# Moving a clamp from VectorE to GpSimd and putting a one-element ScalarE write ahead of each attention exponential

## The chip, the cores and the metric

The kernel runs on one core of one Trainium2 chip. The metric is the device time of one execution in microseconds (us). A core has five engines that each run their own list of instructions in order and meet through semaphores: TensorE (PE, matmuls; its weight loads are shown as PEld), VectorE (DVE), ScalarE (ACT), GpSimd (POOL) and SyncE (SP, which here only issues DMAs). Matmuls write to PSUM, which has eight banks; everything else on the chip lies in SBUF.

## The reference

Two attention blocks with separate inputs, whose results are laid side by side. Each has sequence S = 2048, width D = 640 and 32 heads of 20.

```python
def _A_ref(x, wqkv, wo):            # sliding window of 256
    q, k, v = split(x @ wqkv)       # (B, H, S, 20) each
    scores = einsum("bhqd,bhkd->bhqk", q, k) * 20 ** -0.5
    scores = where((0 <= i - j) & (i - j < 256), scores, -1e9)
    return merge(einsum("bhqk,bhkd->bhqd", softmax(scores), v)) @ wo

def _B_ref(x, wqkv, wo):            # linear attention
    q, k, v = split(x @ wqkv)
    phi = lambda t: where(t > 0, t + 1, exp(t)) + 1e-6
    pq, pk = phi(q), phi(k)
    kv, z = einsum("bhsd,bhse->bhde", pk, v), pk.sum(axis=2)
    num, den = einsum("bhqd,bhde->bhqe", pq, kv), einsum("bhqd,bhd->bhq", pq, z)
    return merge(num / (den[..., None] + 1e-6)) @ wo

concatenate([_A_ref(A), _B_ref(B)], axis=-1)
```

The kernel computes phi(t) as max(t, 0) + min(exp(t) + 1e-6, 1 + 1e-6): the second term is the clamp that the change is about.

## The kernel before

**Units of block A.** The window attention is cut into 90 units: for a piece `s` of 512 queries and a group `g` of four heads there are two or three units, each with up to 512 score columns for each of the four heads. `scores` (line 474) runs a unit: 8 to 16 matmuls (line 483) write S_ps, a tile of four PSUM banks of which there is one; one exponential on ACT (line 491) turns all 128x2048 scores into a tile `p`, of which there are three; one or two `affine_select` instructions on POOL (line 505) set to zero what lies outside the window. `values` (line 516) multiplies `p` by v (line 527) into O_ps, one PSUM bank of which there is one, and after the last unit of a group DVE divides by the row sums (lines 549 and 550). `values` of a unit is issued two units after its `scores` (LAG = 2).

**Fill.** Everything else (the projections of A and B, block B, both output projections) is a generator, `fill` (line 627), of dense matmuls. The loop over the units (line 672) issues `scores` of the unit, `values` of the unit two before, and then so many columns of `fill` as a credit allows, about 3,715 a unit. The order on every engine is what this program order gives; nothing is reordered later. TensorE thus runs, unit by unit: scores, older values, about one and a half dense chains. A dense chain (line 194) is five matmuls that add up in one of three PSUM banks (tile `dense`); DVE, or in `phi` ACT and DVE, has to read a bank before a later chain can write it.

**phi** (line 200) takes a bank `src`: ACT writes `e = exp(src)` (line 203); DVE clamps `e` in SBUF (line 207); DVE adds max(src, 0), which reads the bank a last time (line 210, a `scalar_tensor_tensor`, "the sum" below). The two DVE instructions are not issued at once but kept in `later`, and issued by the next `flush`, that is right behind the next eviction or the next phi's exponential. phi runs 40 times, five at a time: in the four `b_kv(s)` (keys of B, each chain followed by one of v) and the four `b_q(s)` (queries of B).

**Who else uses POOL.** Besides the selects it sets a column of ones in v (lines 309 and 358), masks kv (line 163, once, ten instructions) and issues the DMAs of line 106, 617 and 349, all in one order.

Of the kernel before, what the change touches and what calls it, by code (L numbers as in the profile page):

```python
# [9 lines left out]
P = 128  # L10
ALU = mybir.AluOpType
ACT = mybir.ActivationFunctionType
ENG = mybir.EngineType
BF16 = mybir.dt.bfloat16
# [6 lines left out]
SB = 512  # L21
# [31 lines left out]
def kernel(  # L53
# [10 lines left out]
    nc = tc.nc  # L64
# [4 lines left out]
    scale = float(DH) ** -0.5  # L69
# [5 lines left out]
    def pool(name, bufs, space=None):  # L75
        if space is None:
            return ctx.enter_context(tc.tile_pool(name=name, bufs=bufs))
        return ctx.enter_context(tc.tile_pool(name=name, bufs=bufs, space=space))
# [6 lines left out]
    pp = pool("p", 3)  # L85
# [3 lines left out]
    op1 = pool("o1", 2)  # L89
# [59 lines left out]
    ident = wp.tile([P, P], BF16, name="ident")  # L149
# [26 lines left out]
    def flush():  # L176

        while later:
            later.pop(0)()
# [20 lines left out]
    def phi(dst, src, view=lambda t: t[:]):  # L200

        e = sp.tile([P, SB], BF16, name="e")
        nc.scalar.activation(out=view(e), in_=src, func=ACT.Exp)  # L203
        flush()

        def rest():
            nc.vector.tensor_scalar(  # L207
                out=e[:], in0=e[:], scalar1=1e-6, scalar2=1.0 + 1e-6, op0=ALU.add, op1=ALU.min
            )
            nc.vector.scalar_tensor_tensor(  # L210
                out=dst, in0=src, scalar=0.0, in1=view(e), op0=ALU.max, op1=ALU.add
            )

        later.append(rest)
# [140 lines left out]
    def b_kv(s):  # L355
# [4 lines left out]
        def done(tb, ps):  # L360
            if tb is None:
                phi(pk[:, :, SB:D], ps, lambda t: t[:].rearrange("p (t n) -> p t n", n=P))
            else:
                phi(pk[:, tb, 0:SB], ps[:])
# [45 lines left out]
    def b_q(s):  # L410
        xt = xB[NS + s]
        pq = pqp.tile([P, KT, SB], BF16, name="phi")
        pq_of[s] = pq
        for c in range(KT):
            ps = bank()
            yield from chain(
                ps[:],
                lambda kt: w_sb["B"][:, kt, c * P : (c + 1) * P],
                lambda kt: xt[:, kt, :],
                SB,  # L420
            )
            phi(pq[:, c, :], ps[:])
            yield End(SB)
# [47 lines left out]
    def key(s, rel):  # L471
        return 4 * s + rel

    def scores(s, parts):
        S_ps = sps.tile([P, 4, SB], F32, name="S_ps")
        p = pp.tile([P, 4, SB], BF16, name="p")
        for g, rel, blk, qs in parts:
            kb = key(s, rel)
            kt = k_pad[kb // TPS]
            ko = (kb % TPS) * P  # L480
            q0, n = qs[0][0] * P, len(qs) * P
            for j in range(4):
                nc.tensor.matmul(  # L483
                    S_ps[:, j, blk * P : blk * P + n],
                    lhsT=kt[32 * j : 32 * j + DH, g, ko : ko + P],
                    rhs=q_pad[s][32 * j : 32 * j + DH, g, q0 : q0 + n],
                    start=True,
                    stop=True,
                    tile_position=(32 * j, 0),
                )  # L490
        nc.scalar.activation(out=p[:], in_=S_ps[:], func=ACT.Exp, scale=scale)  # L491
        runs = []
        for _, _, blk, qs in sorted(parts, key=lambda x: x[2]):
            for i, (_, kind) in enumerate(qs):
                if kind == "F":
                    continue
                b = blk + i
                if runs and runs[-1][0] == kind and runs[-1][2] == b:
                    runs[-1][2] = b + 1
                else:  # L500
                    runs.append([kind, b, b + 1])
        for kind, b0, b1 in runs:
            v = p[:, :, b0 * P : b1 * P].rearrange("p j (b q) -> p j b q", q=P)
            sgn = 1 if kind == "D" else -1
            nc.gpsimd.affine_select(  # L505
                out=v,
                in_=v,
                pattern=[[0, 4], [0, b1 - b0], [sgn, P]],
                compare_op=ALU.is_ge,
                fill=0.0,  # L510
                base=0 if kind == "D" else -1,
                channel_multiplier=-sgn,
            )
        return p
# [157 lines left out]
    for i, (okey, first, last, parts) in enumerate(units):  # L672
        p = scores(okey[0], parts)
        if i == 0:
            late_loads()
        pend.append((okey, first, last, parts, p))
        if len(pend) > LAG:
            values(*pend.popleft())
        credit += rate
        credit -= take(credit)  # L680
# [35 lines left out]
```

## Time and profile before

| what | us |
|---|---|
| median of 3 runs (lowest, highest) | 291.31 (289.54, 292.64) |
| the profiled execution's own time | 290.37 |
| its span (first to last instruction of the program) | 288.5 |
| TensorE busy | 273.9 (95%) |
| ScalarE busy | 193.4 (67%) |
| VectorE busy | 183.5 (64%) |
| GpSimd busy | 161.0 (56%) |

All times inside the execution are counted from the span's start. The granted TensorE clock was full throughout. In the groups of instructions a line reads: source line, engine, operation, tiles out<-in, shapes, xcount | busy time of the group, mean ns of one | idle time of the engine just before them <- what ended it. Busy time of TensorE contains pipelining with modelled ends, so 95% does not by itself mean that TensorE is the limit.

Some more numbers of this profile. TensorE waits for DVE to free a dense bank for 0.9 + 0.2 us (line 210), 1.8 us (line 449) and 1.7 us (line 185) in all; it waits 0.5 us for the exponential of line 491. The first exponential starts at 38.65 us and the last at 269.14 us. The clamp on DVE takes 282, 373 and 1409 ns (lowest, median, highest of 40) and 530 on the mean; the sum behind it 692 ns; the exponential of line 203 takes 591 ns. On POOL a select over 512 elements takes 690 ns on the mean, one over 1024 elements 1114 ns.

### The profile page before, as it was taken

How to read it: one execution, taken by the hardware profiler on the slowest of the kernel's cores; microseconds unless marked ns; L12 is line 12 of the kernel's file. 1: busy time of each engine (PE TensorE's matmuls, PEld its weight loads, DVE VectorE, ACT ScalarE, POOL GpSimd, SP SyncE). 2: the span in 40 equal slices, each digit the busy share in tenths (PEclk: the TensorE clock that was granted, in tenths of full speed). 3: DMA queues.
4: the chain of work that ended last, by engine and by line, in shares of the span. 5: the costliest groups of instructions: out<-in, count | busy, mean ns of one | idle time of the engine just before them, and what ended most of it. 6: DMA issues, size and time to landing. Idle time of an engine off the chain costs nothing.

```text
span 288.5 us, 8169 instructions
## 1 busy us (share of the span) xinstructions
PE 273.9 (95%) x3512; PEld 159.1 (55%) x3512; DVE 183.5 (64%) x409; ACT 193.4 (67%) x137; POOL 161.0 (56%) x212
## 2 busy tenths in 40 slices
PE   7999999999999999999999899998999999998995
PEld 7644555665666644565654554444545464545653
DVE  0666646847855744556657884458866887677861
ACT  2000058978889777789888767797688878976402
POOL 2000039657576666776699556666665766665620
PEclk9999999999999999999999999999999999999999
DMA  7997699999173172362062543079755145022486
GB/s 245 291 320 197 166 197 251 269 107 207 36 118 70 24 69 93 94 138 46 2 128 59 113 49 114 4 179 151 129 113 72 70 70 137 2 93 48 130 168 204
DMA packets 66676, 35.91 MB, mean 124 GB/s; under 512 B 50801, under 2 KB 65265, under 8 KB 66641
## 3 DMA queue, kind: packets, MB, share of 16 engines
q1 hardware_dynamic: 63792, 27.04, 49.5%
q0 software_dynamic: 1536, 7.05, 7.7%
q10 hardware_dynamic: 1312, 1.31, 1.4%
q8 instruction: 27, 0.44, 0.6%
q14 instruction: 9, 0.07, 0.1%
HBM read 12.45 MB, written 10.49 MB: 79 GB/s over the span
## 4 chain that ended last, share of the span: by engine, by line
PE 58%; ACT 17%; DVE 9%; issue 6%; DMA 6%; POOL 2%; SPq 0%; ACTq 0%; POOLq 0%
PE dense L194 35%; ACT p L491 14%; PE S_ps L483 10%; PE O_ps L527 9%; DMA k_scr<-st 2%; ACT e L203 2%; DMA kpad<-k_scr 2%; DVE phi L210 2%; PE dense L377 2%; DMA oT<-otokA 2%; PE dense L146 2%; DVE e L207 1%; POOL p L505 1%; DVE osb L185 1%; DVE otokB L449 1%
## 5 line engine op out<-in xcount | busy, mean ns | idle before, releaser
L491 ACT ACTIVATE p<-S_ps 128x2048 bf16<-128x2048 f32 x90 | 169.0, 1878 | 72.9 <-PE S_ps L483 68.2
L505 POOL TENSOR_SCALAR_AFFINE_SELECT p<-p 128x512 bf16<-128x512 bf16 (+2 forms) x178 | 145.1, 838 | 112.3 <-ACT p L491 112.2
L527 PEld LDWEIGHTS <-p 128*128 128x128 bf16 x1440 | 42.4, 96 | 19.7 <-issue 16.2
L527 PE MATMUL O_ps<-vA,p 128*128 128x21 bf16 x1440 | 51.1, 173 | 0.8 <-POOL p L505 0.7
L194 PE MATMUL dense<-wB,xB 128*128 128x320 bf16 (+2 forms) x320 | 49.3, 298 | 0.2 <-DVE phi L210 0.2
L194 PE MATMUL dense<-xA,wA 128*128 128x512 bf16 x200 | 46.1, 379 | 0.0
L185 DVE CAST st<-dense 128x512 bf16<-128x512 f32 x40 | 27.4, 690 | 20.5 <-PE dense L194 18.7
L483 PE MATMUL S_ps<-qpad,kpad 20*128 20x256 bf16 (+2 forms) x736 | 36.1, 269 | 2.9 <-ACT p L491 0.5
L185 DVE CAST osb<-dense 128x512 bf16<-128x512 f32 (+1 forms) x39 | 25.2, 647 | 16.1 <-PE dense L194 16.0
L194 PEld LDWEIGHTS <-xA 128*128 128x128 bf16 x320 | 26.4, 97 | 15.6 <-issue 1.5
L194 PEld LDWEIGHTS <-xB 128*128 128x128 bf16 x320 | 26.1, 97 | 13.3 <-issue 1.2
L483 PEld LDWEIGHTS <-kpad 20*128 20x128 bf16 x736 | 15.0, 92 | 32.4 <-issue 29.2
L194 PEld LDWEIGHTS <-wA 128*128 128x128 bf16 x200 | 18.5, 97 | 19.6
L210 DVE SCALAR_TENSOR_TENSOR phi<-dense,e 128x512 bf16<-128x512 f32 x40 | 27.7, 692 | 1.4
L194 PE MATMUL dense<-woA,oT 128*128 128x512 bf16 (+1 forms) x160 | 25.8, 299 | 2.7 <-DVE osb L185 1.6
L207 DVE TENSOR_SCALAR e<-e 128x512 bf16<-128x512 bf16 x40 | 21.2, 530 | 11.2 <-ACT e L203 11.1
L194 PE MATMUL dense<-xB,wB 128*128 128x512 bf16 x100 | 25.7, 378 | 0.9 <-DVE phi L210 0.8
L194 PE MATMUL dense<-wA,xA 128*128 128x320 bf16 x160 | 24.9, 299 | 1.4 <-DVE otokB L449 0.8
L194 PE MATMUL dense<-woB,xA 128*128 128x512 bf16 (+1 forms) x160 | 25.3, 299 | 0.5 <-PE dense L436 0.4
L203 ACT ACTIVATE e<-dense 128x512 bf16<-128x512 f32 x40 | 23.4, 593 | 0.2 <-PE dense L194 0.2
L185 DVE CAST vB<-dense 128x320 bf16<-128x320 f32 x32 | 15.2, 488 | 11.5 <-PE dense L194 11.1
L549 DVE RECIPROCAL recA<-O_ps 128x16 f32<-128x16 f32 (+1 forms) x34 | 8.5, 250 | 20.8 <-PE O_ps L527 20.7
(35 smaller groups left out, 152.0 us busy)
## 6 DMA issues: line engine op xcount, KB each, us to landing
out_dram<-osb POOLq DMA_DIRECT2D x7, 640.0 KB, 3.9
qpad<-q_scr SPq DMA_DIRECT2D x16, 160.0 KB
kpad<-k_scr SPq DMA_DIRECT2D x16, 160.0 KB
wA<-in_A_wqkv_dram SPq DMA_DIRECT2D x3, 800.0 KB
q_scr<-st SPq DMA_DIRECT2D x3, 640.0 KB
k_scr<-st SPq DMA_DIRECT2D x3, 640.0 KB
wB<-in_B_wqkv_dram SPq DMA_DIRECT2D x2, 800.0 KB
wB<-in_B_wqkv_dram POOLq DMA_DIRECT2D x1, 800.0 KB, 10.8
```

The costliest lines, as they stand in the source:

```text
L146: nc.tensor.matmul(ps[:, 0:P], lhsT=ident[:], rhs=ident[:], start=True, stop=True)
L185: nc.vector.tensor_copy(out=dst, in_=src)
L194: nc.tensor.matmul(dst, lhsT=lhs(kt), rhs=rhs(kt), start=(kt == 0), stop=(kt == KT - 1))
L203: nc.scalar.activation(out=view(e), in_=src, func=ACT.Exp)
L207: nc.vector.tensor_scalar(out=e[:], in0=e[:], scalar1=1e-6, scalar2=1.0 + 1e-6, op0=ALU.add, op1=ALU.min)
L210: nc.vector.scalar_tensor_tensor(out=dst, in0=src, scalar=0.0, in1=view(e), op0=ALU.max, op1=ALU.add)
L377: nc.tensor.matmul(pv, lhsT=pk[:, tb, c * P : (c + 1) * P], rhs=vB[:, tb, a : b + 1, :], start=(tb == 0), stop=(tb == TPS - 1),)
L483: nc.tensor.matmul(S_ps[:, j, blk * P : blk * P + n], lhsT=kt[32 * j : 32 * j + DH, g, ko : ko + P], rhs=q_pad[s][32 * j : 32 * j + DH, g, ...
L491: nc.scalar.activation(out=p[:], in_=S_ps[:], func=ACT.Exp, scale=scale)
L505: nc.gpsimd.affine_select(out=v, in_=v, pattern=[[0, 4], [0, b1 - b0], [sgn, P]], compare_op=ALU.is_ge, fill=0.0, base=0 if kind == "D" el ...
L527: nc.tensor.matmul(O_ps[:, slot, j, :], lhsT=p[:, j, b * P : (b + 1) * P], rhs=v_tok[kb // TPS][:, kb % TPS, 4 * gg + j, :], start=(first ...
L549: nc.vector.reciprocal(out=r[:, 0:n, :, :], in_=O_ps[:, :, :, DH:HV])
```

## The change

The clamp is issued on POOL instead of DVE, and it is issued at once behind the exponential of `phi`, no longer through `later`; the sum stays in `later` and on DVE. The tile `p` becomes two elements wider, and in front of the score matmuls of each unit ACT copies one element (of the identity matrix `ident`) into the first extra element of the new `p`. The exponential writes the first 2048 elements as before. The copy adds 90 instructions to ACT; the clamp takes 40 from DVE and adds 40 to POOL.

```diff
         e = sp.tile([P, SB], BF16, name="e")
         nc.scalar.activation(out=view(e), in_=src, func=ACT.Exp)
+        nc.gpsimd.tensor_scalar(
+            out=e[:], in0=e[:], scalar1=1e-6, scalar2=1.0 + 1e-6, op0=ALU.add, op1=ALU.min
+        )
         flush()
 
         def rest():
-            nc.vector.tensor_scalar(
-                out=e[:], in0=e[:], scalar1=1e-6, scalar2=1.0 + 1e-6, op0=ALU.add, op1=ALU.min
-            )
             nc.vector.scalar_tensor_tensor(
                 out=dst, in0=src, scalar=0.0, in1=view(e), op0=ALU.max, op1=ALU.add
             )
...
         S_ps = sps.tile([P, 4, SB], F32, name="S_ps")
-        p = pp.tile([P, 4, SB], BF16, name="p")
+        p_all = pp.tile([P, 4 * SB + 2], BF16, name="p")
+        p = p_all[:, 0 : 4 * SB].rearrange("p (j q) -> p j q", j=4)
+        nc.scalar.activation(out=p_all[0:1, 4 * SB : 4 * SB + 1], in_=ident[0:1, 0:1], func=ACT.Copy)
...
-        nc.scalar.activation(out=p[:], in_=S_ps[:], func=ACT.Exp, scale=scale)
+        nc.scalar.activation(out=p, in_=S_ps[:], func=ACT.Exp, scale=scale)
```

In the built program the exponential of line 491 waits for TensorE, ScalarE and GpSimd before the change (an event instruction of ACT holds the first two waits, the exponential the third), from the fifth unit on. After it, the one-element copy holds the waits for the old readers and writers of `p`, and the exponential waits for TensorE alone.

## The prediction

> **What bounds the kernel now.** I read the page's first part, then its groups, then ACT's instructions in order of time, then the chain that ended last, and last the timeline of one unit.
>
> ```profile
> PE 273.9 (95%) x3512; PEld 159.1 (55%) x3512; DVE 183.5 (64%) x409; ACT 193.4 (67%) x137; POOL 161.0 (56%) x212
> L491 ACT ACTIVATE p<-S_ps 128x2048 bf16<-128x2048 f32 x90 | 169.0, 1878 | 72.9 <-PE S_ps L483 68.2
> L207 DVE TENSOR_SCALAR e<-e 128x512 bf16<-128x512 bf16 x40 | 21.2, 530 | 11.2 <-ACT e L203 11.1
> ```
>
> TensorE looks full, and ACT waits 68.2 us for scores. But ACT's instructions in order of time (start, duration) show a beat:
>
> ```profile
> 41.02 1.88 ACT L491 ACTIVATE p<-S_ps 128x2048 bf16<-128x2048 f32 x1 [0.50 <-PE S_ps L483]
> 42.80 0.59 ACT L203 ACTIVATE e<-dense 128x512 bf16<-128x512 f32 x1
> 43.40 1.88 ACT L491 ACTIVATE p<-S_ps 128x2048 bf16<-128x2048 f32 x1
> ...
> 51.42 1.88 ACT L491 ACTIVATE p<-S_ps 128x2048 bf16<-128x2048 f32 x1
> 53.20 0.59 ACT L203 ACTIVATE e<-dense 128x512 bf16<-128x512 f32 x1
> 53.88 1.88 ACT L491 ACTIVATE p<-S_ps 128x2048 bf16<-128x2048 f32 x1
> ```
>
> From 51.42 to 53.88 is 2.456 us, and 51 of the 89 intervals of the 90 exponentials go with that beat: there the next scores begin 0.05 us behind the exponential's end. There is one S_ps, so exponential, scores, exponential is a closed loop. In the other 38 intervals TensorE comes to the scores later than that. So two limits alternate, TensorE's own work per unit and this loop, and TensorE has on the mean 0.12 us to spare in the 51. The chain shows what lies between scores and exponential:
>
> ```profile
> 242.13 0.36 PE S_ps L483 x8
> 242.49 0.02 issue
> 242.51 0.04 ACTq L491
> 242.55 0.04 issue
> 242.59 1.89 ACT p L491
> ```
>
> ACTq L491 is the event instruction that holds the wait for the scores. 41.02 to 43.40 is the beat of the first units, whose exponentials wait for TensorE alone: 2.375 us, 0.08 less. Third, phi, in the timeline of one unit:
>
> ```profile
> 73.48 0.59 ACT L203 ACTIVATE e<-dense 128x512 bf16<-128x512 f32 x1
> ...
> 73.65 1.78 POOL L505 TENSOR_SCALAR_AFFINE_SELECT p<-p 128x1024 bf16<-128x1024 bf16 x2 [1.14 <-ACT p L491]
> ...
> 74.11 0.79 DVE L207 TENSOR_SCALAR e<-e 128x512 bf16<-128x512 bf16 x1 [0.59 <-ACT e L203]
> ...
> 74.93 0.69 DVE L210 SCALAR_TENSOR_TENSOR phi<-dense,e 128x512 bf16<-128x512 f32 x1
> 75.68 0.37 PEld L194 LDWEIGHTS <-xB 128*128 128x128 bf16 x3 [0.21 <-issue]
> ```
>
> The sum (line 210) ends at 75.63 and the next chain in the same bank starts at 75.68. I paired each of the 40 sums with the next chain in its bank (the built program tells the bank): 12 chains start 0.05 us behind the sum, four more within 0.26 us. TensorE now waits only about 1 us for it in all, because the sum comes just in time.
>
> **The change, part by part.**
>
> *The exponential's waits.* With TensorE alone to wait for, the loop is 0.08 us shorter. TensorE's spare time caps this: the smaller of 0.083 and what it has to spare, added up over the 51 intervals, is 3.9 us. Some 13 of them will be lost to the stalls below; I count 2.9 us. In the 38 other intervals the gain is nothing, since TensorE comes last.
>
> *The copy of one element.* ACT rows give its fixed part: (1878 - 593) ns over 1536 elements is 0.837 ns each, which leaves 593 - 428 = 165 ns. 90 of them are 15 us of ACT. What it waits for, the values of the unit three before and their selects, stands ahead of the scores on TensorE and is long done. Without a phi it runs in the 0.50 us in which ACT waits for the scores. Behind line 203, which starts 0.10 us before the exponential ends and so ends 0.49 us after it, the copy can start at 0.39 with the same overlap, ends at 0.56 and lets the exponential start at 0.46 to 0.56, against 0.50 when the scores are done. So nothing, up to 0.06 x 40 = 2.4 us where no overlap exists; in three units with two phis it adds some 0.1 us each. A price as low as zero changes nothing, as the wait for scores covers it.
>
> *The clamp leaves DVE.* 21.2 us go from an engine that TensorE waits for 5 to 6 us in all (0.9 and 0.2 behind line 210, 1.8 behind 449, 1.7 behind 185, the rest small). The clamp's 530 ns with 282 at the least is DVE held up beside running selects. What it is worth is counted with the next step, where the sum's start is worked out anew.
>
> *The clamp on POOL.* No row shows it. Nearest are the selects of 512 elements, 690 ns, same bytes in and out; from below the select of 147 elements, 380; from above two selects, 1380. I take 690. The price is not its length but its place: POOL works in order, the selects of the unit's `p` stand in front of it, and they start 0.07 us after the exponential and last 1.36 to 1.83 us, while `e` is ready 0.49 us after the exponential. In the unit above: selects to 75.44, clamp to 76.13, sum (0.06 later, from ACT to POOL 0.07 and to DVE 0.03) from 76.19 to 76.88; it now starts at 74.93. The bank comes free 1.25 us later, and the chain that started at 75.68 waits 1.25 us, and with it everything behind it on TensorE, the next scores too. DVE waits in order as well: evictions and row sums stand behind the sum, but their delay falls into the same stall.
>
> So for each phi I took: end of what stands in front of the clamp on POOL, or of `e` plus 0.07, whichever is later; plus 0.75; less the sum's present start. That is 1.25 us or more in 22 of the 40 and under 0.6 in 17, where `e` or the flush came late anyway. From it I took what the bank had to spare. Where two phis in a row overrun, the second's `e` and selects lie ahead of the first stall, which has given it that time already; I counted the difference only.
>
> | phis | us into the span | overruns added | counted |
> |---|---|---|---|
> | b_kv(0), POOL late from three DMA issues (lines 106, 617) | 41 to 59 | 5.4 | 3.5 |
> | b_kv(1) | 62 to 78 | 2.7 | 1.9 |
> | b_kv(2) | 81 to 98 | 1.3 | 1.25 |
> | b_kv(3) | 126 to 143 | 1.3 | 1.25 |
> | b_q(0), behind the ten instructions of line 163 | 146 to 161 | 4.7 | 3.6 |
> | b_q(1) | 186 to 199 | 4.2 | 2.9 |
> | b_q(2) | 212 to 229 | 3.3 | 2.0 |
> | b_q(3) | 241 to 258 | 0 | 0 |
>
> 16.4 us counted, of 22.8. POOL itself keeps up: selects of 1.36 to 1.83 and a clamp of 0.69 against a beat of 2.46, and values come two units later. The output DMA issues of line 349 (0.77 us, seven) and the memsets (0.7 us, eight) stand in the same order, but where clamps are they are few. SP's queue gets nothing new.
>
> A rule against the change: the Trainium skill, "GPSIMD Engine Reference", section 4.1 "Engine selection", wants elementwise work on VectorE, with one-input work on GpSimd about as fast, and its section 3.1 gives 769 ns for the best loop over 512 elements. By that the clamp would be 0.08 us longer, an estimate that adds some 1 us on 13 stalls. The select's 690 ns is this case's row.
>
> **Sum.** 290.4 (the profiled execution) + 16.4 - 2.9 = 303.9, so **304 us**. The median shown, 291.3, is 0.3% above that execution; against it this is +4.4%. About 1% is what a measurement of this kernel can tell from no change.
>
> **Rivals.**
>
> *Faster: the stalls are absorbed.* Each stall makes the units longer, so later chains could find POOL idle and banks free. If the overruns come to less than 2.9 us the change wins; with none at all and all 51 intervals gaining it is 290.4 - 3.9 = 286.5. For it: half of the 40 banks have over 0.8 us to spare, and DVE loses 21 us of work. Against it: the select in front of the clamp moves with the unit, so the 1.25 us come again in each. A chance of 0.07; 0.07 more that it ends within 1%. The Trainium skill, "Advanced Engine Details and Errata", section "VectorE Performance Modes", has VectorE's two-port instructions and GpSimd block each other on a shared port. The clamp's 282 to 1409 ns on DVE agree, and this would be the reason for such a relief.
>
> *The clamp is slow on POOL.* At 1.38 us each stall grows by 0.69: 13 x 0.69 = 9 us, and POOL then needs 2.74 to 3.2 us in a unit with a phi, more than the beat. 313 us. At 0.38 it is 300. Chance 0.15 for the slow one.
>
> *The copy doesn't do what it says.* If it starts only when ACT has run dry and its own event instruction comes behind that, the exponential is no earlier, and 40 units with a phi are 0.06 later: 290.4 + 16.4 + 2.4 = 309. Chance 0.1.
>
> *The forecast* has 0.61. **Range 294 to 318**: below, half of the counted stalls with the full gain (290.4 + 8.2 - 3.9 = 294.7); above, all 22.8 us of overruns with a clamp between 0.69 and 1.38 (290.4 + 22.8 + 4.5 = 317.7). Slower by over 1%: 0.86.
>
> **What would show it.** Right: 2.375 in place of 2.456 us between exponentials far from any phi (100 to 126, 172 to 186); TensorE's waits for the sum (line 210) up from about 1 to over 10 us; the sum waiting on POOL for most of its 40; the clamp near 0.69 us, starting where a select ends. Wrong: the beat unchanged; waits of TensorE for the sum of under 3 us; clamps that start right behind `e`; or a new wait of the exponential for the copy.

## The result, and the profile after

The changed kernel takes **359.74 us** (median of 4 runs, 355.54 to 360.61) where the kernel before takes 291.07 us (median of 4, 289.54 to 292.64). The ratio is 1.2333, with a 95% interval of 1.2242 to 1.2424. The prediction had the sign, slower, but 304 us and a range up to 318; the loss is five times the one forecast. The profiled execution of the changed kernel took 360.61 us, its span 358.9 us. (Some executions of one and the same kernel, 5 of 12 of the kernel before in one session, come out 2 to 3% longer at a lower granted clock; the ratios given here compare the others.)

From its profile's page: the busy time of each engine, the granted TensorE clock in 40 slices, the shares of the chain that ended last by engine, and three of the groups of instructions.

```profile
PE 300.1 (84%) x3512; PEld 164.9 (46%) x3512; DVE 163.4 (46%) x369; ACT 200.6 (56%) x227; POOL 240.8 (67%) x252
...
PEclk9999985899699879999978799988799869989999
...
PE 46%; POOL 35%; ACT 7%; DVE 5%; issue 4%; DMA 1%; POOLq 0%; ACTq 0%
...
L493 ACT ACTIVATE p<-S_ps 128x2048 bf16<-128x2048 f32 x90 | 168.8, 1875 | 110.4 <-PE S_ps L485 110.3
...
L204 POOL TENSOR_SCALAR e<-e 128x512 bf16<-128x512 bf16 x40 | 76.8, 1920 | 3.4
L210 DVE SCALAR_TENSOR_TENSOR phi<-dense,e 128x512 bf16<-128x512 f32 x40 | 27.7, 692 | 108.5 <-POOL e L204 108.5
```

(The lines after 204 count two higher than before: 491 is now 493, 483 is 485, 505 is 507, 527 is 529.) Four things are to be seen. The clamp (line 204) takes 1920 ns, not 690. The sum (line 210) waits 108.5 us for it. POOL, 2% of the chain before, is 35% of it now. And TensorE is busy 26.2 us longer (300.1 against 273.9) with the same 3512 matmuls, while its granted clock, full throughout before, falls below full in many slices. What POOL's clamp does not do is slow the instructions of other engines: the sum takes 692 ns before and after, the other PSUM reads of VectorE (line 185, 128x512) 690, the exponential 1878 and 1875. So the span's 70.4 us (358.9 - 288.5) are 44.2 us in which TensorE idles and 26.2 us in which it works more slowly.

Who makes TensorE idle, from its waits in the changed kernel (line, what it waited for, us in total, times, longest):

```profile
PE dense L194 <- DVE phi L210: 37.6, 24, 3.5
PE dense L436 <- DVE phi L210: 8.1, 6, 1.8
```

and in the kernel before:

```profile
PE dense L194 <- DVE phi L210: 0.9, 3, 0.5
```

45.7 us for the sum, against 0.9 before (the 0.2 us named beside it above are a part of the 0.9): the idle time is this wait. One of them in order of time (start, duration, what, idle time before):

```profile
118.58 3.23 POOL L507 TENSOR_SCALAR_AFFINE_SELECT p<-p 128x512 bf16<-128x512 bf16 x4
118.74 0.59 ACT L203 ACTIVATE e<-dense 128x512 bf16<-128x512 f32 x1
...
119.28 0.84 PE L194 MATMUL dense<-wB,xB 128*128 128x320 bf16 x5 [1.12 <-DVE phi L210]
...
121.07 0.56 PE L529 MATMUL O_ps<-vA,p 128*128 128x21 bf16 x16
...
121.89 1.92 POOL L204 TENSOR_SCALAR e<-e 128x512 bf16<-128x512 bf16 x1
...
123.84 0.69 DVE L210 SCALAR_TENSOR_TENSOR phi<-dense,e 128x512 bf16<-128x512 f32 x1 [3.52 <-POOL e L204]
...
124.59 1.49 PE L194 MATMUL dense<-wB,xB 128*128 128x320 bf16 x5 [2.54 <-DVE phi L210]
...
127.54 0.60 PE L529 MATMUL O_ps<-vA,p 128*128 128x21 bf16 x16
```

`e` is ready at 119.33, but the selects of two units run first, to 121.81; then come the clamp, the sum, and the dense chain that needs the sum's bank. This is the mechanism of the prediction, with a clamp of 1.92 us in it. TensorE stood idle from 122.05 to 124.59.

With that clamp POOL is also full wherever phis follow one another. POOL's instructions in one such stretch:

```profile
310.20 1.92 POOL L204 TENSOR_SCALAR e<-e 128x512 bf16<-128x512 bf16 x1
312.18 1.85 POOL L507 TENSOR_SCALAR_AFFINE_SELECT p<-p 128x1024 bf16<-128x1024 bf16 x2
314.12 1.92 POOL L204 TENSOR_SCALAR e<-e 128x512 bf16<-128x512 bf16 x1
```

Less than 0.1 us lies between one and the next, and so it is from clamp to clamp in 28 of the 32 cases in which both belong to the same five phis; a unit with one phi then takes 3.50 or 3.92 us, where the beat before was 2.46. The exponential that lets the next selects start waits for scores, the scores for the dense chain before them, that chain for the sum, and the sum for POOL.

The chain at 124.59 shows the second effect: its five matmuls of line 194 take 1.49 us, where five of the same shape took 0.84 us at 119.28. (The 16 matmuls of the values hardly change, 0.56 and 0.60 us.) The windows around it show why. Each of these lines has a start and an end, its length, the busy time of TensorE, of weight loads, VectorE, ScalarE and GpSimd (with instructions), then the granted clock, the DMA share and GB/s:

```profile
119.80:123.20 3.40, 2.00 (x32) 1.02 (x30) 0.52 (x2) 1.96 (x2) 3.25 (x4) 1.00 0.00 0
123.20:126.60 3.40, 2.01 (x11) 1.44 (x11) 1.97 (x4) 0.00 (x0) 2.39 (x3) 0.50 0.00 0
126.60:130.00 3.40, 3.40 (x42) 2.49 (x41) 1.54 (x6) 1.96 (x2) 0.39 (x1) 0.50 1.24 156
130.00:133.40 3.40, 3.40 (x49) 1.54 (x48) 1.85 (x5) 2.04 (x3) 1.90 (x3) 1.00 0.20 42
```

After a window with 1.40 us of idle TensorE the next two are granted half the clock; the full one comes back after a window in which TensorE is busy throughout. In all, 65 us of this execution ran at half clock, none of the profiled execution before.

What the change was to do on ScalarE, it does. Its instructions far from any phi (start, duration, idle time before):

```profile
138.27 1.88 ACT L493 ACTIVATE p<-S_ps 128x2048 bf16<-128x2048 f32 x1 [0.41 <-PE S_ps L485]
140.05 0.19 ACT L478 ACTIVATE p<-ident 1x1 bf16<-1x1 bf16 x1
140.65 1.88 ACT L493 ACTIVATE p<-S_ps 128x2048 bf16<-128x2048 f32 x1 [0.41 <-PE S_ps L485]
```

From 138.27 to 140.65 is about 2.375 us, where before it was 2.456.

Since the start of a kernel is sometimes disturbed by a late load, the experiments below also give the stretch from the first exponential of line 493 to the last: 230.5 us before (38.65 to 269.14), 300.6 us after, so +70.1.

### The profile page after: what moved, and what is told of

Its sections match the earlier page's. It is cut to its first block, busy times and chain, and to the rows that moved or that the text cites. A ratio compares the mean times of both kernels' runs of the same rounds, so it can differ in the third digit from the quotient of the medians.

```text
span 358.9 us, 8254 instructions
## 1 busy us (share of the span) xinstructions
PE 300.1 (84%) x3512; PEld 164.9 (46%) x3512; DVE 163.4 (46%) x369; ACT 200.6 (56%) x227; POOL 240.8 (67%) x252
## 4 chain that ended last, share of the span: by engine, by line
PE 46%; POOL 35%; ACT 7%; DVE 5%; issue 4%; DMA 1%; POOLq 0%; ACTq 0%
PE dense L194 30%; POOL e L204 18%; POOL p L507 16%; ACT p L493 7%; PE S_ps L485 6%; PE O_ps L529 6%; DVE phi L210 2%; PE dense L377 2%; PE dense L146 1%; DMA oT<-otokA 1%; PE dense L436 1%; DVE otokB L449 1%; DVE otokA L552 1%; DVE osb L185 1%; PE dense L130 0%
## 5 line engine op out<-in xcount | busy, mean ns | idle before, releaser
L507 POOL TENSOR_SCALAR_AFFINE_SELECT p<-p 128x512 bf16<-128x512 bf16 (+2 forms) x178 | 147.2, 828 | 98.1 <-ACT p L493 88.7
L194 PE MATMUL dense<-wB,xB 128*128 128x320 bf16 (+2 forms) x320 | 58.4, 325 | 25.0 <-DVE phi L210 23.9
L204 POOL TENSOR_SCALAR e<-e 128x512 bf16<-128x512 bf16 x40 | 76.8, 1920 | 3.4
L210 DVE SCALAR_TENSOR_TENSOR phi<-dense,e 128x512 bf16<-128x512 f32 x40 | 27.7, 692 | 108.5 <-POOL e L204 108.5
L529 PEld LDWEIGHTS <-p 128*128 128x128 bf16 x1440 | 43.0, 97 | 22.8 <-issue 16.2
L194 PEld LDWEIGHTS <-xB 128*128 128x128 bf16 x320 | 28.0, 103 | 43.1 <-issue 30.1
L194 PE MATMUL dense<-xB,wB 128*128 128x512 bf16 x100 | 31.6, 446 | 10.5 <-DVE phi L210 10.5
L485 PE MATMUL S_ps<-qpad,kpad 20*128 20x256 bf16 (+2 forms) x736 | 39.2, 290 | 0.7 <-ACT p L493 0.5
L185 DVE CAST st<-dense 128x512 bf16<-128x512 f32 x40 | 27.5, 690 | 19.8 <-PE dense L194 18.2
L194 PE MATMUL dense<-woA,oT 128*128 128x512 bf16 (+1 forms) x160 | 29.7, 326 | 4.7 <-DVE otokB L449 2.0
L485 PEld LDWEIGHTS <-kpad 20*128 20x128 bf16 x736 | 12.6, 94 | 37.8 <-issue 36.6
L194 PEld LDWEIGHTS <-wA 128*128 128x128 bf16 x200 | 18.6, 98 | 19.8 <-issue 0.3
L478 ACT ACTIVATE p<-ident 1x1 bf16<-1x1 bf16 x90 | 16.9, 188 | 15.4 <-DVE st L185 15.4
L185 DVE CAST vA<-dense 128x320 bf16<-128x320 f32 x32 | 15.6, 491 | 8.7 <-PE dense L194 8.7
```

The source lines that it names most:

```text
L185: nc.vector.tensor_copy(out=dst, in_=src)
L194: nc.tensor.matmul(dst, lhsT=lhs(kt), rhs=rhs(kt), start=(kt == 0), stop=(kt == KT - 1))
L204: nc.gpsimd.tensor_scalar(out=e[:], in0=e[:], scalar1=1e-6, scalar2=1.0 + 1e-6, op0=ALU.add, op1=ALU.min)
L210: nc.vector.scalar_tensor_tensor(out=dst, in0=src, scalar=0.0, in1=view(e), op0=ALU.max, op1=ALU.add)
L478: nc.scalar.activation(out=p_all[0:1, 4 * SB : 4 * SB + 1], in_=ident[0:1, 0:1], func=ACT.Copy)
L485: nc.tensor.matmul(S_ps[:, j, blk * P : blk * P + n], lhsT=kt[32 * j : 32 * j + DH, g, ko : ko + P], rhs=q_pad[s][32 * j : 32 * j + DH, g, ...
```

## The experiments

My theory after the result: POOL's price for the clamp is set by its two operations per element and is 1.92 us; the clamp stands behind the unit's selects, so the bank comes free late; TensorE waits, and through its waits falls to half clock. The rivals: the copy on ScalarE causes part of the loss; POOL's mere work (its shared port with VectorE, or its memory traffic) slows the others; the place behind the selects does not matter, since a clamp so long is late anywhere.

### Only the copy

The clamp is put back on VectorE, in `rest()`, as it was before the change; the copy stays.

```diff
-        nc.gpsimd.tensor_scalar(
-            out=e[:], in0=e[:], scalar1=1e-6, scalar2=1.0 + 1e-6, op0=ALU.add, op1=ALU.min
-        )
         flush()
 
         def rest():
+            nc.vector.tensor_scalar(
+                out=e[:], in0=e[:], scalar1=1e-6, scalar2=1.0 + 1e-6, op0=ALU.add, op1=ALU.min
+            )
```

> Half of the change: the one-element copy stays, the clamp goes back to DVE and into the deferred part, as before the change. Theory A (the copy is worth what the sum said, the clamp on POOL is the whole loss): the beat between exponentials is 2.375 us instead of 2.456 where scores follow at once, TensorE's own work caps it, 286.5 to 288 us by the profiled execution of before (-1.0% to -1.3%). Rival C (the copy costs more than it brings, because ACT is in its way behind line 203): 291 us or more.

Measured: a ratio of 0.9907 to the kernel before, interval 0.9866 to 0.9947, so 291.07 x 0.9907 = 288.4 us, a little short of the 1.0 to 1.3% expected. (The profiled execution of this kernel has one wait of 5.3 us in TensorE's issue, so the beat is read from the price run below, which is this kernel with eight instructions at its end.) There 37 intervals are at 2.375 us and the stretch between first and last exponential is 227.7 us, 2.75 less than before. No stall by the sum takes anything from the gain here, so the figure of the prediction to set beside it is 3.9 us, all 51 intervals gaining, and not 2.9: the copy does what it was said to do, with some 70% of the size. By itself it makes the kernel about 1% faster.

### Only the clamp

The clamp stays on POOL; `p` and its exponential are as before the change.

```diff
-        p_all = pp.tile([P, 4 * SB + 2], BF16, name="p")
-        p = p_all[:, 0 : 4 * SB].rearrange("p (j q) -> p j q", j=4)
-        nc.scalar.activation(out=p_all[0:1, 4 * SB : 4 * SB + 1], in_=ident[0:1, 0:1], func=ACT.Copy)
+        p = pp.tile([P, 4, SB], BF16, name="p")
...
-        nc.scalar.activation(out=p, in_=S_ps[:], func=ACT.Exp, scale=scale)
+        nc.scalar.activation(out=p[:], in_=S_ps[:], func=ACT.Exp, scale=scale)
```

> The other half: the clamp on POOL, without the copy. Theory A: the loss stays whole and the copy's gain is missing: 360 to 364 us, with the beat back at 2.456 us between exponentials far from phi. Rival C (the copy is part of the loss): well under 355 us.

Measured: 356.74 us in one run. The beat is back at 2.456 us; the clamp takes 1918 ns; TensorE waits 35.5 + 8.7 us for the sum. The loss comes with the clamp. The time lies below the 360 to 364 expected, and inside what the changed kernel itself scatters over (355.54 to 360.61), so the copy's gain can't be seen where POOL sets the time. The traces show that the copy even costs something there. In the two kernels without it the second select of a pair starts 0.04 us before the first has ended, in those with it 0.07 us behind; so the clamps here are 3.38 or 3.80 us apart, and 3.50 or 3.92 in the changed kernel. Over its 28 cases that is an estimated 3 us; the stretch between the exponentials is 5.6 us longer with the copy than without (300.6 and 295.0), in one execution each.

### The clamp at the length that was forecast

The clamp works on 144 of the 512 elements, which makes it as long on POOL as the prediction took it to be. The place stays.

```diff
-            out=e[:], in0=e[:], scalar1=1e-6, scalar2=1.0 + 1e-6, op0=ALU.add, op1=ALU.min
+            out=e[:, 0:144], in0=e[:, 0:144], scalar1=1e-6, scalar2=1.0 + 1e-6, op0=ALU.add, op1=ALU.min
```

> The changed kernel with POOL's clamp over the first 144 of 512 elements only; the other 368 are left unclamped, so phi is computed differently there and the output differs. Its place in POOL's order is kept, only its length changes. Theory A (length): if the clamp's time goes with its elements it is about 0.6 to 0.75 us, near the 0.69 us that the forecast took, the overruns are those of the forecast's table, no half clock is granted, and the time is 300 to 306 us. Rival B (place: a clamp behind the selects is late whatever its length, stalls add up to more than the table): 315 us or more.

Measured: a ratio of 1.0635 (1.0552 to 1.0718), a median of 310.12 us. The clamp's tile (duration in ns lowest/median/highest, first and last start):

```profile
L204 POOL TENSOR_SCALAR e<-e x40: 690/692/697, 47.0 to 275.6; 128x144 bf16<-128x144 bf16 x40
```

and TensorE's waits for the sum:

```profile
PE dense L194 <- DVE phi L210: 12.5, 13, 1.7
PE dense L436 <- DVE phi L210: 3.8, 4, 1.2
```

16.3 us in all, where the prediction counted 16.4. Sorted by the rows of its table, the waits are 2.8, 1.7, 1.5, 1.4, 3.3, 2.8, 2.9 and 0 us, where it has 3.5, 1.9, 1.25, 1.25, 3.6, 2.9, 2.0 and 0. So its table held, and not by luck in the total. But the time is 310, not 304, and lies between the two expectations: 13.7 us of the execution ran at half clock, which neither had. With the clamp's length as forecast the forecast would still have been some 6 us low; the other 50 us up to the changed kernel are the clamp's length.

### One operation instead of two

```diff
-            out=e[:], in0=e[:], scalar1=1e-6, scalar2=1.0 + 1e-6, op0=ALU.add, op1=ALU.min
+            out=e[:], in0=e[:], scalar1=1.0, scalar2=None, op0=ALU.min
```

> The changed kernel with one operation in POOL's clamp instead of two (min with 1, without the added 1e-6, which is left out). If the two operations set its length, the clamp falls from 1.92 us to about 1 us and the time to 310 to 325 us. If the instruction costs the same for one operation, it stays at 1.9 us and 360 us.

Measured: 335.62 us in one run, with the clamp in between what the two theories gave:

```profile
L204 POOL TENSOR_SCALAR e<-e x40: 1482/1486/1498, 50.4 to 300.8; 128x512 bf16<-128x512 bf16 x40
```

TensorE waits 25.9 + 4.5 us for the sum. The price falls with one operation, but by a fifth, not by half, so the second operation is only a part of it. The time follows the clamp's length: 310, 336 and 360 us with 0.69, 1.49 and 1.92.

### The sum late without POOL

The copy stays, the clamp is back on VectorE, and VectorE copies the bank three times to the sum's output ahead of each sum. POOL has no work that it did not have before the change.

```diff
         def rest():
+            nc.vector.tensor_scalar(
+                out=e[:], in0=e[:], scalar1=1e-6, scalar2=1.0 + 1e-6, op0=ALU.add, op1=ALU.min
+            )
+            for _ in range(3):
+                nc.vector.tensor_copy(out=dst, in_=src)
```

> The kernel with the copy and the clamp on DVE, where DVE also copies the bank to the sum's output three times ahead of each sum (3 x 0.69 us, overwritten by the sum): every sum is 2.07 us later, nothing is added on POOL. The forecast's recipe without its deduction for shared stalls, with 2.07 us for every phi, adds up to 52.8 us of overruns. Theory A (lateness of the sum is the loss, wherever it comes from; half clock follows TensorE's waits): 330 to 350 us, with half clock granted in stretches after long waits. Rival D (the loss or the half clock belongs to the clamp's work on POOL): no half clock and under 320 us.

Measured: 344.92 us in one run. TensorE's waits for the sum, here line 212:

```profile
PE dense L194 <- DVE phi L212: 32.2, 26, 2.4
PE dense L438 <- DVE phi L212: 8.0, 5, 1.8
```

and two windows of the same kernel (columns as above):

```profile
175.30:178.70 3.40, 1.42 (x21) 0.94 (x22) 3.30 (x6) 1.46 (x3) 3.26 (x5) 1.00 0.28 56
178.70:182.10 3.40, 3.31 (x30) 1.23 (x30) 3.30 (x7) 1.27 (x1) 0.77 (x1) 0.51 0.00 0
```

Nothing was added on POOL, yet the same two effects are there: waits for the sum of 40.2 us, and half clock behind a window with 1.98 us of idle TensorE. So neither needs the clamp's work on POOL; a late sum is enough, and the half clock goes with TensorE's own waits. What makes the sum late here is a full VectorE (3.30 of 3.40 us busy in both windows), as POOL is the full one in the changed kernel.

### The clamp ahead of the selects

The clamp of 144 elements again, but the selects of a unit are issued behind the unit's `fill`, so the clamp no longer stands behind them.

```diff
-        for kind, b0, b1 in runs:
+        def selects():
+          for kind, b0, b1 in runs:
...
-        return p
+        return p, selects
...
         credit -= take(credit)
+        if i:
+            selects()
```

> The kernel of the clamp over 144 elements (0.69 us), with the selects of a unit issued behind the fill of that unit, so that the clamp stands ahead of them in POOL's order; the other 368 elements stay unclamped. Theory A (the place behind the selects makes the clamp late): the sum comes about as early as before the change, the recipe leaves 2 us of overruns, and the time is 288 to 294 us. Rival E (POOL's clamp is late because of its own length and semaphores, the selects matter little): 303 to 310 us, as with the clamp behind them.

Measured: a ratio of 1.0227 (1.0099 to 1.0354), a median of 299.1 us, between the two expectations. TensorE's waits for the sum are gone (0.3 + 0.2 us), but a new one has come:

```profile
PE O_ps L530 <- POOL p L508: 7.6, 14, 1.9
```

The values now wait for the selects, which the clamp has put off. So the place behind the selects was the cause of the waits for the sum, and whichever of the two stands second on POOL is late for someone: about two thirds of the short clamp's loss go (6.35% to 2.27%, with an interval of 1.0 to 3.5%), the rest changes its place.

### No selects

The selects are left out, so the mask on `p` is not applied and POOL has only the full-length clamp beside its small work.

```diff
-        for kind, b0, b1 in runs:
+        for kind, b0, b1 in []:
```

> The changed kernel without the selects on POOL: the window's mask is left out, all else stays, the clamp lasts 1.92 us. It starts 0.07 us after its e instead of behind the selects. By the recipe without the deduction the overruns are 24.4 us: 308 to 316 us under theory A. If the clamp's length alone set the loss (no part for the selects ahead of it), 340 us or more.

Measured: 309.30 us in one run. 7.4 us of this lie ahead of the first exponential, which starts at 46.03 us after a wait for a weight's load; from first to last exponential it is 241.9 us, 11.4 more than before. TensorE waits 11.3 + 3.1 = 14.4 us for the sum. So the 1.92 us alone, with nothing in front of it, cost a third of the waits of the changed kernel (45.7 us); the other two thirds need the selects in front, with which POOL is full. The expectation of 308 to 316 is met only by the late start: without it the time would be about 302, as the recipe's 24.4 us of overruns became 14.4 us of waits.

### POOL's prices

The version with only the copy, and eight instructions on POOL at its very end, on tiles that nobody reads any more (`two` stands for the clamp's two operations; wA and wB are bf16, acc is f32).

```diff
+    g.memset(acc[:, 0:512], 1.0)
+    for n in (128, 256, 512):
+        g.tensor_scalar(out=wA[:, 0, 0:n], in0=wA[:, 0, 0:n], **two)
+    g.tensor_scalar(out=wA[:, 1, 0:512], in0=wA[:, 1, 0:512], scalar1=1.0, scalar2=None, op0=ALU.min)
+    g.tensor_scalar(out=acc[:, 0:512], in0=acc[:, 0:512], **two)
+    g.tensor_copy(out=wB[:, 0, 0:512], in_=wB[:, 1, 0:512])
+    g.tensor_tensor(out=wB[:, 2, 0:512], in0=wB[:, 2, 0:512], in1=wB[:, 3, 0:512], op=ALU.add)
```

> The kernel with the copy alone (clamp on DVE), with eight instructions added at the end of POOL's list, on tiles that are no longer used: the clamp of two operations over 128, 256 and 512 bf16 elements, one operation over 512, two operations over 512 f32 elements, a plain copy of 512 bf16, an addition of two tiles of 512, and a memset. From the clamps of 144 and 512 elements (0.692 and 1.919 us): 212 ns plus 3.33 ns an element, so 0.64, 1.07 and 1.92 us; one operation 1.49 us. If reading and writing bf16 makes the length, f32 is clearly shorter than 1.9 us and the plain copy as long as one operation; if the operations make it, f32 is the same and the copy is near a select's 0.69 us. The kernel's time is that of the copy alone, 286.5 to 289 us, as POOL has some 12 us to spare at the end, and its beat is 2.375 us in at least 35 of 89 intervals.

The three clamps with two operations, by tile (lowest/median/highest, which are those over 128, 256 and 512 elements):

```profile
L694 POOL TENSOR_SCALAR wA<-wA x3: 645/1067/1919, 279.3 to 281.2; 128x128 bf16<-128x128 bf16 x1, 128x256 bf16<-128x256 bf16 x1, 128x512 bf16<-128x512 bf16 x1
```

and the others from POOL's timeline:

```profile
283.20 1.50 POOL L695 TENSOR_SCALAR wA<-wA 128x512 bf16<-128x512 bf16 x1
284.76 1.93 POOL L696 TENSOR_SCALAR kv_acc<-kv_acc 128x512 f32<-128x512 f32 x1
286.73 0.61 POOL L697 COPY wB<-wB 128x512 bf16<-128x512 bf16 x1
287.31 1.15 POOL L698 TENSOR_TENSOR wB<-wB 128x512 bf16<-128x512 bf16 x1
```

The run took 291.99 us, over the 286.5 to 289 expected: the added list starts only at 278.70, behind the last output DMA that POOL issues, and is the last work of the kernel, to 288.5. The clamp's length is a fixed part and a part per element: (1919 - 645) / 384 = 3.32 ns per element, which leaves 645 - 128 x 3.32 = 220 ns. Twice the bytes (f32) cost nothing: 1930. One operation over 512 elements is 1.50 us, a copy of as many elements and bytes 0.61, a select 0.69 (from the profile before). So for the same number of elements the price goes by the kind of instruction, and the bytes don't matter. The number of operations is a part of it (1.50 us for one, 1.92 for two) but not all: an addition of two tiles is one operation on each element as well, and takes 1.15. What else a `tensor_scalar` pays for on POOL is not shown.

### The two effects, added up

For each kernel in which the sum or the values come late: the growth of the stretch from first to last exponential, and what is behind it by the traces. "Waits" is TensorE's waiting for the sum (and with the selects put off, for the selects) over that of before; "half clock" is half of TensorE's busy time in the windows granted half the clock within the stretch, as if at full clock all that work took half as long (the matmuls of the values don't, so this is somewhat too high); "copy" is the -2.75 us of the kernel with the copy alone, carried over to every kernel that has it, where it was not measured.

| kernel | waits | half clock | copy | sum | measured |
|---|---|---|---|---|---|
| changed kernel | 44.9 | 28.9 | -2.75 | 71.0 | 70.1 |
| only the clamp | 43.2 | 22.1 | 0 | 65.3 | 64.6 |
| clamp of 144 elements | 15.3 | 5.7 | -2.75 | 18.3 | 19.8 |
| one operation | 29.5 | 13.6 | -2.75 | 40.3 | 41.8 |
| late sum on VectorE | 39.3 | 17.1 | -2.75 | 53.7 | 54.7 |
| short clamp ahead of the selects | 6.6 | 1.7 | -2.75 | 5.5 | 8.4 |
| no selects | 13.5 | 1.6 | -2.75 | 12.3 | 11.4 |

(In three of these traces, from "only the clamp" to "one operation", 42 of the 3512 matmul records are missing, so their half-clock term is a little low.) In six of the seven the two effects and the copy give the growth within 2 us; for the clamp ahead of the selects 3 us stay unexplained. This is an account of where TensorE's time went; it does not say what each part would give back. Of the 65 us at half clock in the changed kernel, the chain of work that ended last lies on TensorE for 38.5 us; for most of the rest it lies on POOL, ScalarE and VectorE, and there a faster TensorE would only have waited longer. So a full clock could have given back no more than an estimated 19 us (half of the 38.5). The half clock was not taken away by itself: that would need matmuls in TensorE's waits, and all PSUM banks are in use. This was not tried.

## Why the prediction was wrong, and where it was right

**The clamp's price: wrong, and this is the step that failed.** "I take 690", from the select, with 380 and 1380 as the bounds. Measured: 1919 ns, outside the bounds. The select moves the same bytes, and I took that as the likeness that counts. The price run shows that it isn't: f32 costs no more than bf16, and instructions over the same 512 elements cost 611 (copy), 690 (select), 1150 (add of two tiles), 1497 (one operation) or 1919 ns (two). No row of the profile before had a tensor-scalar operation on POOL, so the upper bound of two selects was no bound at all. With the price a second term fails, "POOL itself keeps up". At 1.92 us it doesn't: selects and clamp fill POOL, one unit with a phi takes it 3.50 or 3.92 us, and POOL makes up 35% of the chain. Even at 0.69 us it barely does: 1.83 + 0.69 is 2.52, over the beat of 2.46. The page cited, the Trainium skill, "GPSIMD Engine Reference", section 4.1 "Engine selection", has one-input work on GpSimd about as fast as on VectorE, and its section 3.1 has 769 ns for the best loop over 512 elements. The copy's 611 ns lie below that figure, the clamp's 1919 far above it. The page's advice to keep elementwise work on VectorE is borne out by the clamp's two rows, 530 ns on the mean there and 1919 here.

**The mechanism and the table: right, for the clamp that was forecast.** The selects in front, the late bank, the wait of TensorE are what the trace shows. With the clamp at 0.69 us the table's 16.4 us meet 16.3 measured, row by row to within 0.9 us, though they fall on 17 waits and not on 13. The deduction for shared stalls is rough: the recipe's overruns without it were 22.8, 24.4 and 52.8 us, and the waits of those kernels are 16.3, 14.4 (no selects) and 40.2 (late sum on VectorE), 59 to 76% of them. At 1.92 us the table's way of counting late banks one by one no longer describes the kernel, since POOL is full: the last five phis, b_q(3), for which the table has 0, wait 4.3 us.

**The half clock: missing from the sum.** "290.4 + 16.4 - 2.9" has no term for it, and nor has the rival of a slow clamp. No row of the profile before shows it, since there TensorE hardly waits. With the measured waits and half clock in the forecast's sum, 290.4 + 44.9 + 28.9 - 2.9 = 361.3, against the 360.6 us of the profiled execution: the two terms add up, but they are not two separate causes. At the clamp's forecast length the half clock makes 5.7 us and the forecast is 6 us low; nearly all the rest of the 57 us by which it fell short comes with the clamp's length, more half clock included.

**The exponential's waits: right in kind, smaller in size.** Without POOL's clamp 3.9 us were counted, and 2.75 us and a ratio of 0.9907 measured; the beat is 2.375. Whether any of the 2.9 us is left in the changed kernel no run shows; the run without the copy speaks against it.

**The copy: right on ScalarE.** 165 ns estimated, 188 measured; no wait of the exponential for it is to be seen. The sum has nothing for what it costs on POOL, 0.11 us for each pair of selects.

**The rivals.** "The stalls are absorbed" falls: even without selects TensorE waits 14.4 us for the sum. "The copy doesn't do what it says" falls with the run that has only the copy. "The clamp is slow on POOL" is what happened, and it saw that POOL would need more than the beat. But its price of 1.38 us was too low, and it charged the growth to 13 stalls only: once POOL is full the clamp adds to nearly every phi (the sum waits for POOL in 39 of 40), and TensorE waits 30 times.

**What was to show it.** The beat of 2.375, waits for the sum over 10 us and the sum waiting for POOL came as said. The clamp "near 0.69 us" did not, and this line alone, read from the profile after, would have told the rest.

## What to carry to other kernels

Take an instruction's price on an engine only from a row of the same kind of operation: on POOL it went from 0.61 to 1.92 us for the same 512 elements, and where no such row exists, the range has to be as wide as that. What is moved to an engine that works in order stands behind that engine's queue, and whoever waits for it waits for the queue. Add up what the engine then has to do in one unit and set it beside the unit's time: its share of the whole execution (56% here before) doesn't show that it will be full just where the work is added. Where a change makes a full TensorE wait, look whether 1.4 us or more of idle time fall into one window of 3.41 us, and count something for the clock: in these runs the half clock made between an eighth and two thirds of the waits (1.6 on 13.5 us, 5.7 on 15.3, 28.9 on 44.9).

## What the runs showed of the hardware that was not expected

**The clock falls sooner than it was thought to.** Every stretch at one granted clock in the traces, but for those that the end of the profile cuts off, is a whole number of 3.41 us long, so I take this as the window. I put every window at full clock of the changed kernel and the experiments beside the clock of the next one: behind windows with more than 1.74 us of TensorE idle time in them the next was always at half clock, below 1.37 us never; between the two it went both ways, 12 times half and 15 times full. The Trainium skill, "TensorE: Matmul & The Clock Gate", section "🔬 Part 1: The HAM clock gate (the "warmup" mystery)", says that the clock goes down after at least one idle window of about 3.4 us. The traces agree with the window's length but not with a whole window of idleness: in the stretch shown above, the 1.40 us of idle time in the window from 119.80 were enough. The page's section "A second HAM failure mode: psum-queue depth-cycling" is nearer: short idle times between groups of matmuls are enough there to make the clock swing; it gives no size for them.

**POOL's price goes by the kind of instruction.** A `tensor_scalar` takes about 0.2 us and 3.3 ns per element with two operations, 1.50 us with one over 512 elements; an addition of two such tiles takes 1.15 us, a select 0.69, a copy 0.61. Two operations on f32 take no longer than on bf16.

**A write on one engine can part two instructions on another.** With the one-element copy on ScalarE, the second of two selects on POOL starts 0.07 us behind the first's end; without it, 0.04 us ahead of it. Why is not shown.
